# A Strassen second product whose operand sums, fifth product and first chunk are put in another order

## The chip, the cores and the metric

The kernel runs on one core of one Trainium2 chip. The metric is the time of one execution on the device in microseconds (us), as the median of several runs. Engines are named as in the profile: PE is the matrix engine (PEld its weight loads), DVE the vector engine, ACT the scalar engine, POOL the GpSimd engine, SP the sync engine, which here only starts DMAs. Each engine takes its instructions in the order in which the program gives them, and DMAs are started from the queues of SP, ACT and POOL.

## The reference

Attention over 8 batches of 8 heads, 576 positions and 64 dimensions, then a two-layer block with squared ReLU. Heads 0 to 3 see a sliding window of 32 positions, heads 4 to 7 a dilated one (every fourth position, 32 of them).

```python
scores = (1 / sqrt(64)) * q @ k.T            # per batch and head, masked
attn = exp(scores - max) / sum               # mask: sliding (h < 4) or dilated
x = (attn @ v).transpose(0, 2, 1, 3).reshape(4608, 512)
h = x @ w_in                                 # 512 -> 2048
out = (maximum(h, 0) ** 2) @ w_out           # 2048 -> 512
```

Inputs and output are float32; the kernel multiplies in float16 and sums in float32.

## The kernel before, in words

**Two streams.** For batch b the attention part writes 576 columns of `xT` (512 x 4608, float16). The two matrix products of the second part take 512 tokens at a time: nine chunks, c = 0 to 8. The program is written out by hand: a chunk's products are a Python generator, `pump(n)` takes n steps of it, and the attention of the next batch is recorded between the pumps. So while attention of batch b runs, the products of chunk b - 1 fill PE. Chunks 7 and 8 have no attention beside them.

**First product of a chunk** (`mm1_gen`). For each of 16 blocks of 128 hidden units (`ffc`), four matmuls of 512 columns write a PSUM tile `ph`; ACT applies ReLU into `rt`, and the square goes to `g`, for two blocks at once on DVE, for blocks 14 and 15 apart. One pair of blocks (`BY_ACT`, blocks 6 and 7) is squared by ACT.

**Second product** (`mm2_strassen_gen`, chunks 1 to 8). It is Strassen's scheme with seven products of half size (16 matmuls of 256 columns each) in place of eight. The left operands are blocks of `g`, or four sums of such blocks, `s1` to `s4` in the tile `sm`, made on DVE by `hidden_sums` (`s2` needs `s1`, `s4` needs `s2`). The right operands are blocks of `w_out` or four differences of them (`T`). There are four PSUM tiles: `poa`, `pod`, `pob`, `poc`. The order of the products is a (into `poa`), d (`pod`), b (`pob`), a again, b again, c (`poc`), c again. The second product of c adds to the first in the same PSUM tile, and the value after the first is needed too: DVE adds it to `u3` for the lower half of the output (line 393) before the second may start. The sums of `g` are made in three parts of the eight block pairs: pairs 0 to 3 after block 10, pairs 4 and 5 after block 13, pairs 6 and 7 after block 15 (`SUMS_AT`). Chunk 0 has no Strassen: `mm2_by_rows_gen` makes the four row blocks `po` with 64 matmuls of 512 columns; its results leave in two DMAs (`ot`, line 337), from the POOL queue.

**Attention.** For batches 0 and 1, q and k are loaded, cast to float16 and transposed on PE (`pt`, `pd`). From batch 2 on, `keep_qk` has POOL start four DMAs that write a float16 copy of q and k to DRAM (`dk`, line 184), and SP starts DMA transposes from there into `QKTx` and `QKTd` (lines 194, 196). Scores are `ps` (sliding) and `pz` (dilated); ACT takes the exponential, DVE multiplies by the mask (line 490). The product with v is `pav` or `paw`, DVE normalizes, PE transposes (`px`, `py`) and ACT copies into `xT`.

**The beginning.** PE runs matmuls on zeros (`idle`) between the pieces of attention of batch 0. Then batch 1's inputs are loaded, the first product of chunk 0 runs whole (its 512 tokens need all of batch 0), with batch 1's transposes and scores between its steps; then `mm2_by_rows_gen(0)` with batch 1's `attn_values`. After the second of its steps, DVE sets a one-word tile `hold`; POOL sets it too after that, and only then starts `keep_qk(2)`. This is how POOL's DMAs are kept back until DVE has reached a place.

Of the kernel before, what the change touches and what calls it, by code (L numbers as in the profile page):

```python
# [13 lines left out]
P = 128  # L14
# [3 lines left out]
def kernel(  # L18
# [255 lines left out]
    def hidden_sums(g, sm, i0, i1):  # L274
# [4 lines left out]
        nc.vector.tensor_add(s1, a21, a22)  # L279
        nc.vector.tensor_sub(s2, s1, a11)  # L280
        nc.vector.tensor_sub(s3, a11, a21)
        nc.vector.tensor_sub(s4, a12, s2)


    BY_ACT = (3,)
    SUMS_AT = {10: (0, 4), 13: (4, 6), 15: (6, 8)}

    def relu_squared(c, ffc, g, ph, rts):
# [5 lines left out]
        if i == NK - 1:  # L294
            nc.vector.tensor_mul(g[:, ffc, :], rt[:, o, :], rt[:, o, :])  # L295
        elif o == 1 and i in BY_ACT:
            nc.scalar.activation(g[:, ffc - 1 : ffc + 1, :], rt, ACTF.Square)
        elif o == 1:
            nc.vector.tensor_mul(g[:, ffc - 1 : ffc + 1, :], rt, rt)  # L299

    def mm1_gen(c, g, sm=None):
        xs = xT[:, :, c * TOKC : (c + 1) * TOKC]
        rts = {}
        for ffc in range(NFF):
# [12 lines left out]
            if sm is not None and ffc in SUMS_AT:  # L317
                hidden_sums(g, sm, *SUMS_AT[ffc])
# [20 lines left out]
    def mm2_strassen_gen(c, g, sm):  # L339
# [20 lines left out]
        def part(name):  # L360
            return osb.tile([P, 2, HM], FP32, name=f"{name}{c}", tag="u", bufs=3)
# [23 lines left out]
        yield  # L385
        yield from product(b_, sm[:, 2], T[:, 2], False)
# [3 lines left out]
        yield  # L390
        c_ = bank("poc")
        yield from product(c_, sm[:, 0], T[:, 0], True)
        nc.vector.tensor_add(otl[:, :, HM:DM], c_, u3)  # L393
# [232 lines left out]
    def begin(b, fill, wide=False):  # L626
        for hp in range(2):
            for i in (1, 0):
                t_sliding(b, hp, i, wide)
                fill()  # L630
        for g in range(2):
            s_sliding(b, g)
            fill()
            for i in (1, 0):
                t_dilated(b, g, i, wide, eng=nc.scalar)
                fill()
        for g in range(2):
# [24 lines left out]

    cast_sliding_qk(0, (nc.scalar, nc.scalar, nc.vector, nc.gpsimd))
# [6 lines left out]
    n_idle = [0]  # L670

    def idle():
        n_idle[0] += 1
        idle_matmuls(pj, 5, P)

    begin(0, idle)

    def idle_and_load():  # L680
        idle()
        if n_idle[0] == 15:
            nc.vector.memset(sq[:, :, :, 0:1], 0.0)
            nc.vector.memset(nd_[:, :, :, 0:1], 0.0)

    attn_values(0, idle_and_load)
# [7 lines left out]
    g0 = hidden(0)  # L694
# [90 lines left out]
```

## Time and profile before

| | |
|---|---|
| median of 13 runs | 351.83 us (349.87 to 354.18) |
| the profiled execution | 349.96 us |
| its span in the trace | 348.2 us |
| outside the span | 1.76 us |
| granted clock of PE, mean | 0.97 |
| busy: PE, DVE, ACT, POOL | 304.9, 205.5, 184.0, 48.4 us |
| moved by DMA | 47.89 MB in 82767 packets |

A row of the profile's groups gives the line, the engine and the operation, output and inputs by the program's names, the shape, how often, then the busy time and the mean of one in ns, then the idle time of the engine just before such instructions and who ended it. A row of the timeline has the start and the duration in us ahead of that. PE's busy time is counted from pipelined matmuls: one of 512 columns is shown with some 380 ns, but 64 of them in a row take 13.98 us.

### The profile page before, as it was taken

To read this page: it belongs to the slowest core of one execution; us is meant where nothing else is said; L and a number is where in the kernel's file an instruction comes from. 1 tells how busy PE (TensorE), PEld (TensorE's weight loads), DVE (VectorE), ACT (ScalarE), POOL (GpSimd) and SP (SyncE) were. 2 spreads that over 40 slices of the span, in tenths; PEclk is the share of its full clock that TensorE was granted. 3 is DMA by queue.
4 is the path that set the end of the run, shared out by engine and by line. 5 is a ranking of instruction groups with operands and counts; after the bars stand their busy time and mean duration, and the time that the engine had idled before them with its cause. 6 is when DMAs were issued, how large, how long until landed. Compare 5 with 4: busy or idle time off the path is not lost.

```text
span 348.2 us, 6958 instructions
## 1 busy us (share of the span) xinstructions
PE 304.9 (88%) x2876; PEld 199.0 (57%) x2876; DVE 205.5 (59%) x420; ACT 184.0 (53%) x311; POOL 48.4 (14%) x83
## 2 busy tenths in 40 slices
PE   6979869996989979897989798979897989899893
PEld 2865445542675459445944496448743874575482
DVE  4484565465972597359735854496538852933632
ACT  2644792378527942794279424962397227404710
POOL 4441752004004000400030002100000000000000
PEclk9869999998999999999999899998999999999999
DMA  8999999799996994599549962997110011003003
GB/s 185 206 203 242 200 181 218 180 189 200 215 187 183 206 228 51 145 199 199 102 136 198 208 102 78 222 188 158 60 63 0 2 57 65 0 2 120 2 0 121
DMA packets 82767, 47.89 MB, mean 138 GB/s; under 512 B 67760, under 2 KB 78512, under 8 KB 82352
## 3 DMA queue, kind: packets, MB, share of 16 engines
q1 hardware_dynamic: 74516, 25.99, 39.1%
q0 software_dynamic: 6848, 19.80, 26.1%
q10 hardware_dynamic: 1372, 1.67, 1.7%
q8 instruction: 22, 0.36, 0.4%
q14 instruction: 9, 0.07, 0.1%
HBM read 39.85 MB, written 16.52 MB: 162 GB/s over the span
## 4 chain that ended last, share of the span: by engine, by line
PE 42%; DVE 25%; ACT 16%; DMA 8%; issue 6%; SPq 1%; POOL 0%; ACTq 0%; DVEq 0%
PE ph L307 11%; PE poa L349 7%; PE pob L349 7%; ACT rt L293 6%; PE pod L349 5%; DVE g L299 5%; ACT AT L489 4%; PE poc L349 4%; DMA QKTx<-dk 3%; DVE x_d L551 3%; DVE AT L490 3%; DMA dk<-in_k_dram 3%; DVE sm L280 2%; ACT vd L145 2%; DMA sq<-in_k_dram 2%
## 5 line engine op out<-in xcount | busy, mean ns | idle before, releaser
L307 PE MATMUL ph<-xT,wi 128*128 128x512 f16 x576 | 133.0, 382 | 2.9 <-ACT rt L293 1.2
L293 ACT ACTIVATE rt<-ph 128x512 f16<-128x512 f32 x144 | 82.3, 609 | 22.8 <-PE ph L307 22.4
L307 PEld LDWEIGHTS <-wi 128*128 128x128 f16 x576 | 54.5, 98 | 66.2 <-issue 6.6
L299 DVE TENSOR_TENSOR g<-rt 128x1024 f16<-128x1024 f16 x54 | 38.7, 720 | 54.7 <-ACT rt L293 54.5
L349 PEld LDWEIGHTS <-sm 128*128 128x128 f16 x512 | 47.2, 98 | 14.6 <-issue 9.8
L349 PEld LDWEIGHTS <-g 128*128 128x128 f16 x384 | 37.1, 101 | 24.8 <-DVE g L295 12.5
L349 PE MATMUL poa<-wo,g 128*128 128x256 f16 x256 | 35.6, 278 | 14.5 <-DVE g L295 10.8
L349 PE MATMUL pob<-T,sm 128*128 128x256 f16 x256 | 32.5, 272 | 0.0
L621 ACT COPY xT<-py 128x576 f16<-128x576 f16 x16 | 10.2, 638 | 40.3 <-PE py L615 40.3
L603 ACT COPY xT<-px 128x576 f16<-128x576 f16 x16 | 10.2, 640 | 39.0 <-PE px L597 39.0
L490 DVE TENSOR_TENSOR AT<-AT,maskp 128x576 f16<-128x576 f16 x32 | 18.6, 585 | 19.5 <-ACT AT L489 18.3
L365 POOL DMA_DIRECT2D out_dram<-otl x6 | 4.5, 756 | 169.8 <-DVE otl L393 152.1
L489 ACT ACTIVATE AT<-pz 128x576 f16<-128x576 f32 x32 | 19.5, 695 | 15.7 <-PE pz L536 15.7
L349 PE MATMUL poc<-wo,sm 128*128 128x256 f16 x128 | 16.3, 272 | 8.8 <-DVE otl L393 8.8
L551 DVE TENSOR_TENSOR x_d<-paw,rcp_d 72x512 f16<-72x512 f32 x32 | 22.0, 687 | 1.1
L489 ACT ACTIVATE AT<-ps 128x576 f16<-128x576 f32 x32 | 19.2, 662 | 0.0
L435 PE MATMUL pj<-zz 128*128 128x128 f16 (+1 forms) x124 | 18.1, 295 | 1.2 <-DVE zz L208 1.2
L349 PE MATMUL pod<-T,g 128*128 128x256 f16 x128 | 18.4, 297 | 0.0
L551 DVE TENSOR_TENSOR x_p<-pav,rcp_p 96x512 f16<-96x512 f32 x24 | 16.5, 687 | 0.8
L349 PE MATMUL poc<-T,sm 128*128 128x256 f16 x128 | 16.2, 272 | 0.0
L322 PE MATMUL po<-wo,g 128*128 128x512 f16 x64 | 15.8, 379 | 0.0
L550 DVE RECIPROCAL rcp_d<-paw 72x8 f32<-72x8 f32 x32 | 6.4, 199 | 15.5 <-PE paw L582 15.5
(89 smaller groups left out, 341.5 us busy)
## 6 DMA issues: line engine op xcount, KB each, us to landing
sv<-in_v_dram SPq DMA_DIRECT2D x40, 128.0 KB, 10.3
sd<-in_v_dram SPq DMA_DIRECT2D x7, 512.0 KB, 8.5
dk<-in_k_dram POOLq DMA_DIRECT2D x12, 288.0 KB, 8.0
dk<-in_q_dram POOLq DMA_DIRECT2D x12, 288.0 KB, 9.1
out_dram<-otl POOLq DMA_DIRECT2D x6, 512.0 KB, 3.3
out_dram<-otu POOLq DMA_DIRECT2D x6, 512.0 KB, 4.1
wi<-in_moe_w_in_dram POOLq DMA_DIRECT2D x2, 1024.0 KB, 10.9
wo<-in_moe_w_out_dram POOLq DMA_DIRECT2D x4, 512.0 KB, 9.8
```

What stands on the lines that cost most here:

```text
L145: nc.scalar.copy(o, i)
L293: nc.scalar.activation(rt[:, o, :], ph[:], ACTF.Relu)
L299: nc.vector.tensor_mul(g[:, ffc - 1 : ffc + 1, :], rt, rt)
L307: nc.tensor.matmul(ph, wi[:, dmk, ffc * P : ffc * P + P], xs[:, dmk, :], start=(dmk == 0), stop=(dmk == NDM - 1),)
L322: nc.tensor.matmul(po, g[:, ffc, t * P : (t + 1) * P], wo[:, ffc, :], start=(ffc == 0), stop=(ffc == NFF - 1),)
L349: nc.tensor.matmul(acc[:, t, :], lhs[:, k, t * P : (t + 1) * P], rhs[:, k, :], start=(first and t == 0 and k == 0), stop=(k == NK - 1), sk ...
L435: nc.tensor.matmul(pj[:, 0:cols], zz[:, 0:P], zz[:, 0:cols], start=True, stop=True)
L489: nc.scalar.activation(AT[:, u, 0:UW], ps[:, :, 0 : UW // 2], ACTF.Exp, scale=scale)
L490: nc.vector.tensor_mul(AT[:, u, 0:UW], AT[:, u, 0:UW], mask)
L551: nc.vector.tensor_tensor(out=x[0:w], in0=pv[:, :, :, 0:D], in1=rcp[0:w].unsqueeze(3).to_broadcast([w, 2, HH, D]), op=ALU.mult,)
L603: nc.scalar.copy(xT[:, 0:2, t0 : t0 + 288], px[:, 0:UW].rearrange("x (c t) -> x c t", c=2),)
L621: nc.scalar.copy(xT[:, 2:4, t0 : t0 + 288].rearrange("x c (i r) -> x c i r", r=DIL), py[:, 0:UW].rearrange("x (c r i) -> x c i r", c=2, r= ...
```

## The change

Two things are changed in the products, and the beginning is written anew.

- The four sums of pairs 0 to 3 are recorded one at a time, after blocks 8, 9, 10 and 11. Those of pairs 4 to 7 come all four after block 15. The pair that ACT squared is squared by DVE.
- In the second product, the first product of c comes before the second of b; ACT copies its result to SBUF (`v5`), and the output's lower half is made from `v5`. The pool that holds `s1`, `u2`, `u3` has four buffers, for `v5`.
- Chunk 0's first product is made in two parts, tokens 0 to 287 and 288 to 511 (`mm1_part_gen`). The first part starts when the attention values of the first 288 positions of batch 0 are there; the rest of that batch's attention is recorded between its steps. The casts of batch 0's v on POOL change places (dilated first, then the loads of `w_in`, then sliding); batch 1's casts go from POOL to ACT and DVE; `w_out` is loaded after a `hold`; the dilated scores of batch 1 move into `mm2_by_rows_gen(0)`, with larger pumps; the loads of v for batch 2 wait for a memset on DVE; in batch 2 four steps more of chunk 1 are pumped ahead of the scores.

```diff
@@ hidden_sums, relu_squared
-        nc.vector.tensor_add(s1, a21, a22)
-        nc.vector.tensor_sub(s2, s1, a11)
-        nc.vector.tensor_sub(s3, a11, a21)
-        nc.vector.tensor_sub(s4, a12, s2)
-    BY_ACT = (3,)
-    SUMS_AT = {10: (0, 4), 13: (4, 6), 15: (6, 8)}
+        yield nc.vector.tensor_add(s1, a21, a22)
+        yield nc.vector.tensor_sub(s2, s1, a11)
+        yield nc.vector.tensor_sub(s3, a11, a21)
+        yield nc.vector.tensor_sub(s4, a12, s2)
...
-        elif o == 1 and i in BY_ACT:
-            nc.scalar.activation(g[:, ffc - 1 : ffc + 1, :], rt, ACTF.Square)
         elif o == 1:
             nc.vector.tensor_mul(g[:, ffc - 1 : ffc + 1, :], rt, rt)
+    def mm1_part_gen(c, g, t0, t1):
+        xs = xT[:, :, c * TOKC + t0 : c * TOKC + t1]
...
@@ mm1_gen
-            if sm is not None and ffc in SUMS_AT:
-                hidden_sums(g, sm, *SUMS_AT[ffc])
+            if sm is not None and ffc >= NFF // 2:
+                if ffc == NFF // 2:
+                    sums = hidden_sums(g, sm, 0, NK // 2)
+                if ffc == NFF - 1:
+                    sums = hidden_sums(g, sm, NK // 2, NK)
+                for _ in sums:
+                    if ffc < NFF - 1:
+                        break
@@ mm2_strassen_gen
+        c_ = bank("poc")
+        yield from product(c_, sm[:, 0], T[:, 0], True)
+        v5 = part("v5")
+        nc.scalar.copy(v5, c_)
+        yield
         yield from product(b_, sm[:, 2], T[:, 2], False)
         u3 = part("u3")
         nc.vector.tensor_add(u3, b_, s1)
         nc.vector.tensor_add(otl[:, :, 0:HM], d_, u3)
-        yield
-        c_ = bank("poc")
-        yield from product(c_, sm[:, 0], T[:, 0], True)
-        nc.vector.tensor_add(otl[:, :, HM:DM], c_, u3)
+        nc.vector.tensor_add(otl[:, :, HM:DM], v5, u3)
         put(1, otl, out_eng)
@@ the beginning
-    cast_sliding_v(nc.gpsimd, 2, 0, 2)
+    cast_dilated_v(nc.gpsimd, 2)
     load_w_in()
-    cast_sliding_v(nc.gpsimd, 2, 2, NB)
-    cast_dilated_v(nc.gpsimd, 2)
+    cast_sliding_v(nc.gpsimd, 2)
...
     load_sliding_qk(1)
     load_v(1)
     load_dilated_qk(1)
-    cast_sliding_qk(1, (nc.gpsimd,) * 4)
-    load_w_out()
-    cast_sliding_v(nc.gpsimd, 2)
-    cast_dilated_v(nc.gpsimd, 2)
     g0 = hidden(0)
-    pending.append(mm1_gen(0, g0))
-    pump(22)
-    begin(1, lambda: pump(1))
+    pending.append(mm1_part_gen(0, g0, 0, 288))
...
+    pump(1000)
+    pending.append(mm1_part_gen(0, g0, 288, TOKC))
+    pump(2)
+    nc.vector.memset(hold, 0.0)
+    nc.gpsimd.memset(hold, 0.0)
+    load_w_out()
+    pump(1)
+    cast_sliding_qk(1, (nc.scalar, nc.vector, nc.scalar, nc.vector))
+    pump(2)
+    transposes_and_scores(1, lambda: pump(1))
     pump(1000)
+    cast_v(nc.scalar)
     pending.append(mm2_by_rows_gen(0, g0))
-    pump(4)
+    pump(3)
+    scores_dilated(1, lambda: pump(3))
...
         if n_val[0] == 2:
             nc.vector.memset(hold, 0.0)
+            nc.vector.memset(sv[:, :, :, 0:1], 0.0)
+            nc.vector.memset(sd[:, :, :, 0:1], 0.0)
     attn_values(1, rows_and_load, True)
     nc.gpsimd.memset(hold, 0.0)
     dk = keep_qk(2)
@@ batch 2
             load_v(b + 1)
-            pump(4)
+            pump(8)
```

The rows below are the built programs' orders, in which `x2` stands for two equal instructions in a row and the number behind a tile's name tells its buffers apart.

On DVE, the end of the first product of chunk 2 (the first chunk with full attention beside it), from the square of a pair of blocks to that of blocks 14 and 15 (line 295 before, 292 now); lines 279 to 282 are the sums `s1` to `s4`, lines 490 and 515 the masks. Before:

```order
L299 TENSOR_TENSOR g_1587<-rt_5_1705 128x1024
L490 TENSOR_TENSOR AT<-AT,maskd 128x576 x2
L299 TENSOR_TENSOR g_1587<-rt_6_1745 128x1024
L279 TENSOR_TENSOR sm_1588<-g_1587 128x512
L280 TENSOR_TENSOR sm_1588<-sm_1588,g_1587 128x512
L281 TENSOR_TENSOR sm_1588<-g_1587 128x512
L282 TENSOR_TENSOR sm_1588<-g_1587,sm_1588 128x512
L295 TENSOR_TENSOR g_1587<-rt_7_1763 128x512 x2
```

Now:

```order
L294 TENSOR_TENSOR g_1676<-rt_4_1762 128x1024
L280 TENSOR_TENSOR sm_1677<-sm_1677,g_1676 128x1024
L281 TENSOR_TENSOR sm_1677<-g_1676 128x1024
L294 TENSOR_TENSOR g_1676<-rt_5_1796 128x1024
L282 TENSOR_TENSOR sm_1677<-g_1676,sm_1677 128x1024
L515 TENSOR_TENSOR AT<-AT,maskd 128x576 x2
L294 TENSOR_TENSOR g_1676<-rt_6_1834 128x1024
L292 TENSOR_TENSOR g_1676<-rt_7_1848 128x512 x2
L279 TENSOR_TENSOR sm_1677<-g_1676 128x1024
```

The four half-length sums that stood between the square of blocks 12 and 13 and those of 14 and 15 are gone from there; the whole-length ones of the first half stand singly between earlier squares.

On DVE again, the end of the second product of chunk 2, from the normalization of the values (`x_d`) to the upper half's last sum; `otl` and `otu` are the output tiles. Before:

```order
L388 TENSOR_TENSOR u_1974<-pob_1867,s_1822 128x512
L389 TENSOR_TENSOR otl_1778<-pod_1824,u_1974 128x2x256
L550 RECIPROCAL rcp_d_0_1987<-paw_1_0_1977 72x8
L551 TENSOR_TENSOR x_d_0_1986<-paw_1_0_1977,rcp_d_0_1987 72x512
L550 RECIPROCAL rcp_d_1_2009<-paw_1_1_1999 72x8
L551 TENSOR_TENSOR x_d_1_2008<-paw_1_1_1999,rcp_d_1_2009 72x512
L393 TENSOR_TENSOR otl_1778<-poc_1990,u_1974 128x2x256
L398 TENSOR_TENSOR otu_1777<-poc_1990,u_1897 128x2x256
```

Now:

```order
L575 RECIPROCAL rcp_d_1_2093<-paw_1_1_2083 72x8
L576 TENSOR_TENSOR x_d_1_2092<-paw_1_1_2083,rcp_d_1_2093 72x512
L416 TENSOR_TENSOR u_2104<-pob_1952,s_1907 128x512
L417 TENSOR_TENSOR otl_1863<-pod_1909,u_2104 128x2x256
L418 TENSOR_TENSOR otl_1863<-v_2060,u_2104 128x2x256
L423 TENSOR_TENSOR otu_1862<-poc_2030,u_1982 128x2x256
```

The sum that read `poc` reads ACT's copy `v` now, and the three sums of the lower half stand together behind the last normalization.

On POOL, the place where batch 2's q and k are started (`dk`, line 184), with the outputs of chunk 0 (`ot`, line 337 before, 360 now) and `hold`. Before:

```order
L135 DMA wo<-in_moe_w_out_dram 128x4x512 x4
L147 CAST vp<-sv 128x8x64 x3
L147 CAST vd<-sd 128x8x64 x4
L712 MEMSET hold 128x1
L184 DMA dk_1038<-in_k_dram 16x9216
L184 DMA dk_1038<-in_q_dram 16x9216
L184 DMA dk_1038<-in_k_dram 16x9216
L184 DMA dk_1038<-in_q_dram 16x9216
L337 DMA out_dram<-ot_0_1059 128x2x512
L337 DMA out_dram<-ot_2_1071 128x2x512
```

Now:

```order
L739 MEMSET hold 128x1
L135 DMA wo<-in_moe_w_out_dram 128x4x512 x4
L360 DMA out_dram<-ot_0_1112 128x2x512
L761 MEMSET hold 128x1
L184 DMA dk_1143<-in_k_dram 16x9216
L184 DMA dk_1143<-in_q_dram 16x9216
L184 DMA dk_1143<-in_k_dram 16x9216
L184 DMA dk_1143<-in_q_dram 16x9216
L360 DMA out_dram<-ot_2_1162 128x2x512
```

The first output of chunk 0 stands ahead of `hold` and of the four copies now, where both outputs stood behind them.

More of the change, by code (lines that the diff above doesn't have):

```diff
@@ L689 @@
     load_dilated_qk(1)
[L690 to L697 removed]
+    g0 = hidden(0)
+    pending.append(mm1_part_gen(0, g0, 0, 288))
+    zs = []
+    for a in range(2):
+        pump(1)
+        zs.append(av_dilated(0, 1, a))
+    pump(1)
+    x_sliding(0, 1, xs, False)
+    pump(2)
+    x_dilated(0, 1, zs, False)
+    pump(1000)
[3 more added lines that the diff above has]
+    nc.gpsimd.memset(hold, 0.0)
+    load_w_out()
+    pump(1)
+    cast_sliding_qk(1, (nc.scalar, nc.vector, nc.scalar, nc.vector))
+    pump(2)
+    transposes_and_scores(1, lambda: pump(1))
     pump(1000)
+    cast_v(nc.scalar)
     pending.append(mm2_by_rows_gen(0, g0))
[L700 removed]
+    pump(3)
+    scores_dilated(1, lambda: pump(3))
     n_val = [0]
[L702 removed]
     def rows_and_load():
```

56 lines of the change are left out of this document (42 added, 14 removed).

## The prediction, on record before the result

> **What bounds the kernel now.** I read the engines' shares first, then PE's groups with their idle time, then the timeline where that idle time lies, the granted clock by stretches, and the chain of waits at the beginning. The engines' line of the page:
>
> ```profile
> PE 304.9 (88%) x2876; PEld 199.0 (57%) x2876; DVE 205.5 (59%) x420; ACT 184.0 (53%) x311; POOL 48.4 (14%) x83
> ```
>
> PE carries the run, and no other engine comes near. So a change pays where PE stands still. Over the whole run two groups of the second product show it:
>
> ```profile
> L349 PE MATMUL poa<-wo,g 128*128 128x256 f16 x256 | 35.6, 278 | 14.5 <-DVE g L295 10.8 <-DVE g L299 3.8
> L349 PE MATMUL poc<-wo,sm 128*128 128x256 f16 x128 | 16.3, 272 | 8.8 <-DVE otl L393 8.8
> ```
>
> 14.5 us are lost before `poa` (the first product of a waits for squares) and 8.8 us before the second product of c (it waits until DVE has read `poc`): 1.8 and 1.1 us in each of eight chunks. In the timeline, chunk 3's first wait:
>
> ```profile
> 153.58 1.00 DVE L490 TENSOR_TENSOR AT<-AT,maskp 128x576 f16<-128x576 f16 x2 [2.15 <-ACT AT L489]
> ...
> 158.25 0.82 PE L349 MATMUL poa<-wo,g 128*128 128x256 f16 x6
> ...
> 158.45 0.60 ACT L293 ACTIVATE rt<-ph 128x512 f16<-128x512 f32 x1 [0.20 <-PE ph L307]
> 159.08 0.68 DVE L299 TENSOR_TENSOR g<-rt 128x1024 f16<-128x1024 f16 x1
> 159.69 0.42 DVE L279 TENSOR_TENSOR sm<-g 128x512 f16<-128x512 f16 x1
> 159.82 0.28 PE L349 MATMUL poa<-wo,g 128*128 128x256 f16 x1 [0.76 <-DVE g L299]
> 161.15 0.75 DVE L295 TENSOR_TENSOR g<-rt 128x512 f16<-128x512 f16 x2
> 161.62 0.28 PE L349 MATMUL poa<-wo,g 128*128 128x256 f16 x1 [1.52 <-DVE g L295]
> ```
>
> PE does six of the first eight matmuls, then waits for the squares of blocks 12 and 13, and again for block 14. ACT's last ReLU ends at 159.05, so block 14's input (one ReLU earlier) was there by 158.45. DVE was late: between 159.69 and 161.15 it made sums that nobody needed yet. DVE had idled 2.15 us before 153.58.
>
> The two chunks without attention, and the end:
>
> ```profile
> 302.52 1.16 PE L349 MATMUL poa<-wo,g 128*128 128x256 f16 x9 [1.34 <-DVE g L295]
> ...
> 341.69 1.91 PE L349 MATMUL poc<-wo,sm 128*128 128x256 f16 x16 [0.78 <-DVE otl L393]
> 343.63 0.76 DVE L402 TENSOR_TENSOR otu<-poc,u 128x256 f32<-128x256 f32 x2 [2.00 <-PE poc L349]
> ```
>
> **Sums and squares, per chunk.** The durations:
>
> ```profile
> L299 DVE TENSOR_TENSOR g<-rt 128x1024 f16<-128x1024 f16 x54 | 38.7, 720 | 54.7 <-ACT rt L293 54.5
> L280 DVE TENSOR_TENSOR sm<-sm,g 128x1024 f16<-128x1024 f16 x8 | 5.5, 692 | 0.3
> L389 DVE TENSOR_TENSOR otl<-pod,u 128x512 f32<-128x512 f32 x8 | 5.5, 691 | 0.3
> L384 ACT COPY otu<-poa 128x512 f32<-128x512 f32 x8 | 4.7, 585 | 16.4 <-PE poa L349 16.4
> ```
>
> The four sums of 159.69 to 161.15 (1.46 us) leave the path. The first half's sums (4 x 0.69) move up by some two blocks, one into the idle 2.15 us; DVE gains one square there (0.72). With one sum (0.69) less in the way, and with the mask of 153.58 some 0.4 us earlier because ACT squares nothing ahead of it, DVE comes to blocks 12 and 13 at about 158.0 instead of 159.08, and without the 1.46 us it squares block 14 right behind, done at 159.1; PE wants it at about 159.0. So 0.1 to 0.4 us of the 2.28 stay; I take 0.3 per chunk: 14.5 - 8 x 0.3 = **12.1 us gained**. Nothing is gained if DVE is behind for another reason (a rival below); the most is 14.5. The second half's sums now cost 2.8 us in a row behind the last square. Their first reader is the third product, two products (32 matmuls) later; `s2` is the second of the four, 1.4 us in. Behind them on DVE wait the mask and the normalizations of the values, whose PSUM pair PE needs back: 1.1 us later against the squares, which are 2 us earlier. Bounds 0 and 0.5 us, I take 0.2 in six chunks with attention: **-1.2**.
>
> **The fifth product.** PE's wait before the second product of c goes: between the end of c's first product and its second lie 16 matmuls of b, some 1.9 us by the row of 341.69, and ACT's copy takes 0.59 like the one on line 384. **+8.8 us.** If ACT were late by more than 1 us, part came back; it waits 16.4 us for PE before the sibling copy, so it is idle there. In the last chunk the three sums of the lower half (3 x 0.69 after b) now run during c's last 1.9 us, and the last two pieces (0.76) start some 0.5 us later: **-0.5**.
>
> **The clock follows the waits.** Stretches, with PE's granted clock third from the end:
>
> ```profile
> 190.00:196.00 6.00, 4.46 (x23) 2.06 (x22) 5.93 (x13) 3.92 (x8) 0.00 (x0) 1.00 1.08 204
> 197.70:200.70 3.00, 3.00 (x16) 2.07 (x15) 1.64 (x5) 1.37 (x3) 0.00 (x0) 0.50 1.13 255
> ...
> 234.90:238.70 3.80, 3.80 (x30) 2.92 (x28) 2.10 (x6) 0.94 (x2) 0.00 (x0) 0.55 0.93 206
> ```
>
> Twice the clock falls to half right behind the two waits of a chunk (before 196, PE was busy 4.46 of 6 us). That costs 3.0 x 0.5 + 3.8 x 0.45 = 3.2 us, and without the waits it should not happen: **+3.2** (0 to 3.2). [...]
>
> **The beginning** is where I expect a loss. The chain that brings batch 2's keys and queries:
>
> ```profile
> 57.02 1.03 POOL dk L184 x2
> 58.05 8.96 DMA dk<-in_k_dram
> 67.03 2.13 SPq L194
> 69.26 12.13 DMA QKTx<-dk
> 81.53 0.67 PE ps L517 x12
> ```
>
> and the timeline beside it:
>
> ```profile
> 56.78 0.10 POOL L712 MEMSET hold<- 128x1 f32 x1 [8.23 <-DVE hold L708]
> ...
> 68.46 0.77 POOL L337 DMA_DIRECT2D out_dram<-ot  x1 [9.31 <-ACT ot L334]
> 69.11 9.23 PE L307 MATMUL ph<-xT,wi 128*128 128x512 f16 x42
> ...
> 85.02 0.53 POOL L184 DMA_DIRECT2D dk<-in_k_dram  x1
> 95.00 5.72 SPq L194 DMA_TRANSPOSE QKTx<-dk  x2
> ```
>
> Copies start at 57.02, transposes at 67.03, and PE, which begins chunk 1 at 69.11 and runs out at 78.3, waits until 81.53. In the new order of POOL's queue the first output of chunk 0 (`ot_0`) stands ahead of `hold` and the copies. It is complete only 0.65 us before chunk 0 ends (68.46 against 69.11), and POOL waits for it in order: here it already did, 9.31 us. So the copies cannot start before about the end of chunk 0 plus 0.1 us, some 11.5 us later than now.
>
> Does chunk 0 end earlier? At the beginning:
>
> ```profile
> 15.15 1.52 POOL L128 DMA_DIRECT2D wi<-in_moe_w_in_dram  x2
> ...
> 18.06 2.28 POOL L147 CAST vd<-sd 128x512 f16<-128x512 f32 x4
> ...
> 31.02 9.23 PE L307 MATMUL ph<-xT,wi 128*128 128x512 f16 x42 [0.29 <-ACT xT L621]
> 36.76 3.53 POOL L147 CAST early<-sq 96x768 f16<-96x768 f32 x4 [9.25 <-DMA sq<-in_k_dram]
> ...
> 40.09 0.42 PE L460 MATMUL pt<-ident,early 96*128 96x96 f16 x6
> ...
> 51.68 0.31 PE L536 MATMUL pz<-QKTd 64*128 64x72 f16 x8 [2.43 <-ACT AT L489]
> ```
>
> The first part of the product can start before 31.02, since of the ten value steps of batch 0 four now come behind its start; I estimate 4 us. But batch 1's transposes need its q and k, which landed at 36.76, and the loads of `w_in` ahead of them now stand behind four casts (2.28 us). The casts, halved between ACT and DVE, take 1.8 us where POOL took 3.53. Both together leave the transposes near 40. At that place 20 matmuls of 512 columns remained, 10,240 columns; now 11 blocks of 4 x 224, 9,856. So the early start is spent waiting. Behind it ACT casts v, in three instructions, ahead of the exponentials that `pz` waits for, which makes the wait of 2.43 rather longer; row products lie around it. I take chunk 0's end at 68.5, between 66.5 and 70.5.
>
> From the copies' start to the scores it takes 24.5 us in the first case (57.02 to 81.53); in the second, 10.0 (85.02 to 95.00), then half of 5.72 and the landing:
>
> ```profile
> QKTx<-dk SPq DMA_TRANSPOSE x2, 5.7
> ```
>
> which is 18.6. The first shared the DMA engines with both outputs of chunk 0, the next one with one of them: I take 21. Scores at 68.6 + 21 = 89.6, 8.1 us later. Two blocks more are pumped ahead of them, 8 matmuls at 9.23/42 = 0.22, 1.8 us of PE time that is saved behind. **-6.3 us**, bounds -1.9 (end at 66.5, 18.6 us) and -11.8 (70.5, 24.5 us).
>
> **Sum.** 12.1 - 1.2 + 8.8 - 0.5 + 3.2 - 6.3 = 16.1 us off the profiled execution's 349.96: 333.9. That execution is the second shortest of the 13; most of their scatter I put down to dips of the clock, of which fewer remain, so I add nothing: **334 us**. Its own bounds: gains between 16 and 25, loss between 2 and 12, so 327 to 346 at the extremes.
>
> **Rivals.**
> (A) The beginning costs nothing: q and k of batch 1 come early enough that chunk 0 ends by 63, and the scores come at 82 to 84. For it speaks the start 4 us earlier, against it that the loads decide and `w_in` is later. It gives 334 - 6 = 328.
> (B) DVE takes half back. In the stretch before 196 it is busy 5.93 of 6 us, the chunk shrinks by 3 us, and the longer block of sums, the masks and the normalizations stand in one queue. If the values' PSUM tiles come back late in each chunk, half of the 22.4 us of steady gain goes: 334 + 11 = 345. Against it speaks that DVE's share over all is 59%.
> (C) Slower: keys and queries become late in every chunk, since POOL starts the copies for the next batch only behind the last output of the chunk before.
>
> ```profile
> 127.17 0.98 PE poa L349 x8
> ...
> 162.27 0.98 PE poa L349 x8
> ```
>
> A chunk takes 35.1 us by these rows of the chain, shortened some 32, and from the copies' start to the scores that use them lies at least one chunk. Copy and transposes take 18.6 to 24.5 us, so a reserve of 7 us stays. It decides from 32 us on; at 39 five chunks would lose 7 each, 334 + 35 = 369, and it is slower than before from 36 on.
> (D) The product's order changes nothing because the waits only change their name (block 14 then waits for ACT): only the fifth product's 8.8 less the loss of 6.3, some 347. ACT loses a square per chunk and its ReLU for block 14 was in time, so this too is unlikely.
>
> **How the numbers follow.** The forecast 0.62, A 0.13, B 0.15, C 0.04, D 0.06. The likeliest case alone is 329 to 340. The range reaches to A below and into B above: 327 to 343. About 0.5% (1.8 us) is what a measurement of this kernel can tell from no change; below 350.1 lie all but C and a small part of D: faster 0.94, same 0.02, slower 0.04.
>
> **What would show it.** The idle time before `poa` should fall from 14.5 to under 4 us, the one before the second product of c to under 1; no half clock near the middle of the run. POOL's row for `ot_0` should show a long wait, the first copy for batch 2 should start at 66 to 71, and PE should wait 8 to 14 us before the first `ps` on `QKTx`. It is wrong if the copies start near 57, if chunk 0 ends before 64, if a chunk with attention still takes over 34 us, or if PE waits for `QKTx` again in later chunks.

## The result and the profile after

| | before | after |
|---|---|---|
| median | 351.17 us of 48 runs (347.33 to 355.24) | 330.97 us of 11 runs (330.01 to 333.45) |
| ratio | | 0.945, 95% interval 0.943 to 0.948 |
| profiled execution, its span | 349.96, 348.2 us | 330.57, 328.8 us |
| a chunk with attention beside it | 35.1 us | 31.85 us |

The ratio compares the means without the few slower executions of the kernel before, so it is not the quotient of the two medians. The changed kernel is 5.5% faster, 3.0 us below the forecast of 334 and inside its range. PE's groups of the second product and of the two places that wait for attention, in the changed kernel (line 372 is 349 of before, 542 is 517, 640 is 615; the columns are busy time and mean ns, then idle time and what ended it):

```profile
L372 PE MATMUL poa<-wo,g 128*128 128x256 f16 x256 | 32.6, 273 | 0.0
L372 PE MATMUL poc<-wo,sm 128*128 128x256 f16 x128 | 16.3, 273 | 0.0
L372 PE MATMUL poc<-T,sm 128*128 128x256 f16 x128 | 16.2, 272 | 2.1 <-ACT otu L407 2.1
L607 PE MATMUL paw<-vd,AT 128*128 128x65 f16 x256 | 13.4, 194 | 1.2 <-DVE x_d L576 0.7 <-DVE x_p L576 0.6
L640 PE MATMUL py<-ident,x_d 72*128 72x72 f16 x128 | 7.2, 197 | 1.3 <-DVE x_d L576 1.1
L542 PE MATMUL ps<-QKTx 64*128 64x96 f16 x144 | 5.7, 216 | 4.9 <-DMA QKTx<-dk 4.9
```

Both waits of before, 14.5 and 8.8 us, are gone. In their place stand a wait of 2.1 us before the first product of c, some 1.9 us more before `paw` and `py` (0.4 and 0.2 before the change), and a longer wait for batch 2's transposed keys (4.9 us for 3.2). The chain of waits shows the chunk's period, from the second eight matmuls of `poa` in one chunk to those of the next two:

```profile
128.33 0.98 PE poa L372 x8
...
160.17 0.98 PE poa L372 x8
...
192.03 0.98 PE poa L372 x8
```

In the middle the granted clock (third column from the end) no longer falls; the stretches that held the two dips of before read 0.72 there and now:

```profile
196.00:202.00 6.00, 5.55 (x75) 4.89 (x74) 3.44 (x10) 1.76 (x3) 0.00 (x0) 1.00 0.93 186
234.00:240.00 6.00, 6.00 (x74) 4.96 (x73) 4.90 (x9) 3.12 (x4) 0.77 (x1) 1.00 0.02 3
```

The timeline of the changed kernel where batch 2's keys and queries are brought:

```profile
57.48 4.70 SPq L106 DMA_DIRECT2D sv<-in_v_dram  x6
...
66.80 0.72 POOL L360 DMA_DIRECT2D out_dram<-ot  x1 [25.67 <-ACT ot L357]
...
67.55 0.53 POOL L184 DMA_DIRECT2D dk<-in_k_dram  x1
...
76.07 5.80 SPq L194 DMA_TRANSPOSE QKTx<-dk  x2
...
84.58 0.67 PE L542 MATMUL ps<-QKTx 64*128 64x96 f16 x12 [4.88 <-DMA QKTx<-dk]
```

Chunk 0 ends at 67.61, the copies start at 67.55, and the first scores of chunk 1 come at 84.58, where they came at 81.53. Behind that wait the clock is at half, by the view of stretches:

```profile
80.00:82.00 2.00, 0.00 (x0) 0.00 (x0) 2.00 (x5) 0.52 (x2) 0.00 (x0) 1.00 1.09 240
82.00:84.00 2.00, 0.00 (x0) 0.00 (x0) 0.68 (x2) 0.00 (x0) 0.00 (x0) 0.86 1.19 237
84.00:86.00 2.00, 1.42 (x14) 0.76 (x15) 0.28 (x1) 0.96 (x2) 0.18 (x1) 0.50 1.06 204
...
90.00:92.00 2.00, 2.00 (x19) 1.27 (x15) 1.44 (x4) 1.87 (x4) 1.85 (x4) 0.93 0.90 204
```

Worked out from the mean of a stretch, the clock is at half from 83.4 to 90.3, and once more from 110.8 to 114.2. The kernel before had one such stretch there, from 81.3 to 84.7.

**Where the time came from.** Up to chunk 1's first scores the changed kernel is 3.05 us later (84.58 against 81.53), up to chunk 2's 3.8 (117.83 against 114.05). From there to the end it takes 210.97 us instead of 234.15, 23.2 less. Together that is the 19.4 us between the spans.

### The profile page after: what moved, and what is told of

Its sections match the earlier page's. It is cut to its first block, busy times and chain, and to the rows that moved or that the text cites. A ratio compares the mean times of both kernels' runs of the same rounds, so it can differ in the third digit from the quotient of the medians.

```text
span 328.8 us, 7031 instructions
## 1 busy us (share of the span) xinstructions
PE 300.6 (91%) x2920; PEld 200.6 (61%) x2920; DVE 207.0 (63%) x409; ACT 188.3 (57%) x331; POOL 38.9 (12%) x73
## 4 chain that ended last, share of the span: by engine, by line
PE 71%; DMA 11%; ACT 10%; DVE 2%; issue 2%; SPq 1%; POOL 1%; ACTq 0%; DVEq 0%
PE ph L324 28%; PE poa L372 9%; PE pob L372 9%; PE poc L372 7%; DMA wi<-in_moe_w_in_dram 4%; PE pod L372 4%; PE po L345 3%; ACT vd L145 3%; DMA sq<-in_k_dram 2%; ACT vp L145 2%; DMA dk<-in_k_dram 2%; PE ph L302 2%; PE paw L607 2%; PE pav L593 2%; PE ps L542 2%
## 5 line engine op out<-in xcount | busy, mean ns | idle before, releaser
L324 PE MATMUL ph<-xT,wi 128*128 128x512 f16 x512 | 119.6, 388 | 1.9 <-ACT rt L290 1.6
L290 ACT ACTIVATE rt<-ph 128x512 f16<-128x512 f32 x128 | 73.8, 602 | 23.5 <-PE ph L324 19.3
L324 PEld LDWEIGHTS <-wi 128*128 128x128 f16 x512 | 49.5, 100 | 61.7 <-issue 8.1
L372 PEld LDWEIGHTS <-g 128*128 128x128 f16 x384 | 35.9, 98 | 5.9
L372 PE MATMUL poa<-wo,g 128*128 128x256 f16 x256 | 32.6, 273 | 0.0
L628 ACT COPY xT<-px 128x576 f16<-128x576 f16 x16 | 10.2, 640 | 30.7 <-PE px L622 30.7
L515 DVE TENSOR_TENSOR AT<-AT,maskp 128x576 f16<-128x576 f16 x32 | 15.4, 482 | 11.9 <-ACT AT L514 10.5
L646 ACT COPY xT<-py 128x576 f16<-128x576 f16 x16 | 10.2, 638 | 18.6 <-PE py L640 18.5
L302 PE MATMUL ph<-xT,wi 128*128 128x288 f16 (+1 forms) x128 | 16.9, 272 | 2.6 <-DMA wi<-in_moe_w_in_dram 1.0
L575 DVE RECIPROCAL rcp_d<-paw 72x8 f32<-72x8 f32 x32 | 6.5, 203 | 19.5 <-PE paw L607 19.4
L515 DVE TENSOR_TENSOR AT<-AT,maskd 128x576 f16<-128x576 f16 x32 | 13.8, 465 | 5.2 <-ACT AT L514 4.8
L576 DVE TENSOR_TENSOR x_p<-pav,rcp_p 96x512 f16<-96x512 f32 x24 | 16.5, 687 | 0.8
```

Source lines behind the costliest of these rows:

```text
L290: nc.scalar.activation(rt[:, o, :], ph[:], ACTF.Relu)
L302: nc.tensor.matmul(ph[:, 0 : t1 - t0], wi[:, dmk, ffc * P : ffc * P + P], xs[:, dmk, :], start=(dmk == 0), stop=(dmk == NDM - 1),)
L324: nc.tensor.matmul(ph, wi[:, dmk, ffc * P : ffc * P + P], xs[:, dmk, :], start=(dmk == 0), stop=(dmk == NDM - 1),)
L372: nc.tensor.matmul(acc[:, t, :], lhs[:, k, t * P : (t + 1) * P], rhs[:, k, :], start=(first and t == 0 and k == 0), stop=(k == NK - 1), sk ...
L515: nc.vector.tensor_mul(AT[:, u, 0:UW], AT[:, u, 0:UW], mask)
L576: nc.vector.tensor_tensor(out=x[0:w], in0=pv[:, :, :, 0:D], in1=rcp[0:w].unsqueeze(3).to_broadcast([w, 2, HH, D]), op=ALU.mult,)
```

## The experiments

Theory at the start: the two edits of the products bring what the prediction says and lose nothing to each other, and the new beginning costs about 6 us because the copies of batch 2's q and k stand behind an output in POOL's queue. Each edit was first made alone on the kernel before. Where the beginning's loss was larger than the theory allowed, it was taken apart.

### The sums and squares alone

The kernel before with the new `hidden_sums`, its new places, and DVE's square for blocks 6 and 7:

```
-    BY_ACT = (3,)
-    SUMS_AT = {10: (0, 4), 13: (4, 6), 15: (6, 8)}
...
+            if sm is not None and ffc >= NFF // 2:
+                if ffc == NFF // 2:
+                    sums = hidden_sums(g, sm, 0, NK // 2)
+                if ffc == NFF - 1:
+                    sums = hidden_sums(g, sm, NK // 2, NK)
```

> The kernel before with the sums and squares of the change alone (first half of the sums one by one after blocks 8 to 11, second half after block 15, all squares on DVE). My account: the idle time before poa goes from 14.5 us to under 1, the 8.8 us before the second product of c stay, and the two half-clock stretches near 197 and 235 us go because the waits ahead of them go: 14.5 + 0 to 3.2 us less, so 333.5 to 337. Rival, the waits only change their name (blocks 14 and 15 wait for ACT, or DVE is late for another reason): 343 or more. Rival on the clock, the dips do not hang on these waits: the idle time falls by 14 us but two half-clock stretches stay in the middle, 336 to 338.

Measured: 326.88 us, ratio 0.928 (0.924 to 0.933), 24.7 us less than before in the same job and 6.6 below the expected range. This edit alone beats the whole change. The groups of this kernel:

```profile
L350 PE MATMUL poa<-wo,g 128*128 128x256 f16 x256 | 32.4, 273 | 0.0
L350 PE MATMUL poc<-wo,sm 128*128 128x256 f16 x128 | 16.3, 272 | 8.8 <-DVE otl L394 8.8
```

The wait before `poa` is gone entirely, and the group's busy time fell too, from 35.6 to 32.4. Idle and busy together are 17.7 us less, where the prediction had 12.1. The chunk's period is 32.7 (120.55 to 153.25), and the clock stays whole from 56 us to PE's last matmul. Between the two spans lie 22.4 us: what the 17.7 leave is mostly the clock, whose three stretches at half behind 80 us are gone, and chunk 1's first scores, at 79.7 for 81.53. The waits before `paw` and `py` are 0.4 and 0.2, as before.

### The fifth product alone

```
+        c_ = bank("poc")
+        yield from product(c_, sm[:, 0], T[:, 0], True)
+        v5 = part("v5")
+        nc.scalar.copy(v5, c_)
...
-        nc.vector.tensor_add(otl[:, :, HM:DM], c_, u3)
+        nc.vector.tensor_add(otl[:, :, HM:DM], v5, u3)
```

> The kernel before with the fifth product early and copied by ACT, alone. My account: the 8.8 us before the second product of c go, about 2.1 us come back as a new wait of c's first product for ACT's copy of poa (as in the changed kernel), the 14.5 us before poa stay: 343.5 to 346. The half-clock stretches behind the poa waits should stay, one to three of them. Rival, c's first product finds its PSUM tile free here and nothing comes back: 341 to 343.

Measured: 343.34 us, ratio 0.975 (0.971 to 0.980), 8.2 us less than before in the same job and 0.2 below the expected range. Its groups:

```profile
L349 PE MATMUL poa<-wo,g 128*128 128x256 f16 x256 | 34.9, 274 | 16.4 <-DVE g L295 11.8 <-DVE g L299 4.6
L349 PE MATMUL poc<-wo,sm 128*128 128x256 f16 x128 | 16.3, 272 | 0.0
L349 PE MATMUL poc<-T,sm 128*128 128x256 f16 x128 | 16.2, 272 | 2.1 <-ACT otu L384 2.1
```

The 8.8 us go. The wait for `otu`, which is ACT's copy of `poa` out of PSUM, comes with this edit and not with the sums: c's first product now stands one product earlier and takes the slot that this copy frees, 0.42 us in each of five chunks. The wait before `poa` is 1.9 us longer than in the kernel before.

### Both, with the old beginning

> The kernel before with sums, squares and the fifth product, and the old beginning. My account, in which the new beginning loses 3 to 4 us by the place of the second chunk's scores: faster than the changed kernel, 326 to 329. Rival, the new beginning is worth its place (the early start of chunk 0's product pays): 331 or more.

The edit is the two above together. Measured: **321.23 us**, ratio 0.913 (0.907 to 0.918), 4.8 below the expected range. This is 9.7 us below the changed kernel, which differs from it only in the beginning. The two agree from chunk 2 on: the period is 31.86 us here (118.89 to 150.75) and 31.85 there. In the one, chunk 2's second eight matmuls of `poa` run at 118.89, in the other at 128.33; 9.4 of the 9.8 us between the spans are there. The timeline of this kernel, to be read against the one of the changed kernel above:

```profile
55.94 0.54 POOL L184 DMA_DIRECT2D dk<-in_k_dram  x1
...
65.06 7.20 SPq L194 DMA_TRANSPOSE QKTx<-dk  x2
...
77.19 0.43 PE L520 MATMUL ps<-QKTx 64*128 64x96 f16 x12
```

No wait for keys stands before these scores, and the clock is whole from 16 us to PE's last matmul. Chunk 0 ends at 68.03: the new beginning, which starts the first product 2.6 us earlier (25.52 against 28.09 here), ends chunk 0 only 0.4 us earlier.

### The new beginning alone

The kernel before with `mm1_part_gen`, the new beginning and `pump(8)`.

> The kernel before with the new beginning alone. My account: the copies of batch 2's q and k start near 67.5 us in place of 57, PE waits some 5 us for QKTx, chunk 1 runs behind by 3 to 4 us from there to the end: 353 to 356. Rival, the new beginning gains: below 349.

Measured: 354.03 us, ratio 1.009 (1.005 to 1.013): slower by 0.9%, as expected. The first scores of chunk 1 come at 87.2 against 81.53. So the beginning costs some 3 us beside the old products and 9.7 beside the new ones. In the profiled executions the old beginning itself is not the same, though the programs differ there only by a square and a few sums of chunk 1 on DVE: the transposes of `QKTx` took 14.5 us (before), 13.2 (sums alone), 11.8 (fifth product alone) and 10.7 (both), and the first scores came at 81.53, 79.7, 77.9 and 77.19. These 4.3 us (81.53 to 77.19), read from one execution each, are most of the difference between the two prices. Why the transposes vary stays open.

### The copies ahead of the first output

The changed kernel with `hold` and the copies recorded at the second value step:

```
             nc.vector.memset(sd[:, :, :, 0:1], 0.0)
+            nc.gpsimd.memset(hold, 0.0)
+            dks.append(keep_qk(2))
...
-    nc.gpsimd.memset(hold, 0.0)
-    dk = keep_qk(2)
```

> The changed kernel with POOL's hold and the four copies of batch 2's q and k recorded at the second step of batch 1's values, so ahead of the first output of chunk 0 in POOL's queue. My account, the output in front of the copies is what the beginning costs: copies at about 57.5 us, QKTx there at 77 to 81, PE waits under 2.5 us before the first scores in place of 4.9, the long half-clock stretch behind that wait shrinks or goes, 321 to 324. Rival, the loads of v for batch 2, which now run at the same time as the copies, hold the transposes back: 328 or more.

Measured: 329.31 us, ratio 0.939 (0.934 to 0.945). The theory falls, in this form; the rival, loads that hold the transposes back, fits. The timeline of this kernel:

```profile
58.65 6.91 SPq L106 DMA_DIRECT2D sv<-in_v_dram  x6
58.85 0.54 POOL L184 DMA_DIRECT2D dk<-in_k_dram  x1
...
68.35 0.37 SPq L114 DMA_DIRECT2D sd<-in_v_dram  x1
...
68.82 14.59 SPq L194 DMA_TRANSPOSE QKTx<-dk  x2
...
86.11 0.67 PE L542 MATMUL ps<-QKTx 64*128 64x96 f16 x12 [5.23 <-DMA QKTx<-dk]
```

The copies start 8.7 us earlier than in the changed kernel, but the scores come 1.5 us later. The transposes started 7.3 us earlier and needed 17.3 us in place of 8.5. Ahead of them in SP's queue, and beside the copies, are the loads of batch 2's values. The new beginning lets them start only at 58 us, behind DVE's two `memset`s of `sv` and `sd`; in the old one they were started from 44.62.

### The order of the casts and the loads of `w_in`

The changed kernel with the casts of batch 0's v in the old order, so that the loads of `w_in` are started earlier:

```
-    cast_dilated_v(nc.gpsimd, 2)
+    cast_sliding_v(nc.gpsimd, 2, 0, 2)
     load_w_in()
-    cast_sliding_v(nc.gpsimd, 2)
+    cast_sliding_v(nc.gpsimd, 2, 2, NB)
+    cast_dilated_v(nc.gpsimd, 2)
```

> The changed kernel with the old order of batch 0's casts on POOL, so that w_in is loaded some 1.7 us earlier. My account: PE's wait of 1.0 us for w_in goes, but batch 1's q and k and the copies behind the output decide, so 329.5 to 331. Rival, the loads of w_in set the beginning: 328 or less.

Measured: 329.44 us, ratio 0.942 (0.935 to 0.948), which overlaps the changed kernel's. The first scores are at 84.33 against 84.58. PE's wait of 1.0 us for `w_in` is gone, as expected, and the time is at the lower edge of the expected range. This order is not where the beginning's loss lies.

### Uneven steps between the value pieces, with the copies ahead

The copies ahead, as above, and the steps between the value pieces of later batches dealt unevenly:

```
-        attn_values(b, lambda: pump(2))
+        steps = iter((2, 2, 2, 2, 2, 0, 4, 2, 2, 2))
+        attn_values(b, lambda: pump(next(steps)))
```

> As e5_early, and in the chunks with attention the first product of c is pumped one piece of attention later and whole, so that a transpose and one product of values stand between poa's last matmul and it. My account, c waits for the PSUM tile that ACT's copy of poa sets free (0.42 us in each of five chunks): 2.1 us shrink to under 1, so 1 to 1.5 us under e5_early. Rival, the wait moves on to the products of values (their PSUM pair): no difference within 0.7 us, or slower.

Measured: 329.12 us, 0.938 (0.934 to 0.942). The wait before c's first product fell from 2.1 to 0.8 us over the run; against the run with the copies ahead (329.31) the total did not move by what can be told.

### The square given back to ACT

The changed kernel with blocks 6 and 7 squared by ACT again.

> The changed kernel with the square of blocks 6 and 7 given back to ACT. My account, the places of the sums are what gained and the square fell into idle time of DVE: 330 to 332, as the changed kernel, idle time before poa still under 1.5 us. Rival, the square's move carries a part of it, since ACT then lags behind PE: 333 or more.

Measured: 333.04 us, 0.949 (0.943 to 0.955), at the edge of the rival's range and not in that of the account; the interval overlaps the changed kernel's. Its group of `poa`:

```profile
L374 PE MATMUL poa<-wo,g 128*128 128x256 f16 x256 | 34.3, 273 | 0.4
```

0.4 us of idle and 1.7 of busy time come back, 2.1 together, and the period is 32.09 us (132.21 to 164.30 in the chain), 0.24 longer. The median is 2.1 higher too, but in the profiled execution 3.3 us lie in the first scores already (87.85), so the time alone proves nothing. By the rows, the order of the sums carries the gain and the square moved to DVE adds some 2 us.

### The loads of batch 2's values released, with the copies ahead

The kernel with the copies ahead, less the two `memset`s that hold the loads:

```
-            nc.vector.memset(sv[:, :, :, 0:1], 0.0)
-            nc.vector.memset(sd[:, :, :, 0:1], 0.0)
```

> The changed kernel with the copies at the second value step (as in the run that moved them) and without the two memsets of sv and sd at that step, which hold the loads of batch 2's values until 57 to 58 us. What the memsets write is written again by the loads, so the work is whole. Theory, loads held: the loads then start behind ACT's casts of the values of batch 1, at 48 to 52 us, in the stretch 52 to 58 us where the transfers stand idle; the transposes no longer queue behind them (in the run with early copies the loads' issue lasted from 58.65 to 68.72, and the transposes took 17 us); they start at 66 to 69 and take 8 to 11 us, the first scores of chunk 1 at 76 to 80 against 86.1, no half clock there, and the median is 319 to 324. Rival, transposes slow whenever they come beside the outputs of chunk 0 and the copies: first scores at 84 or later and 327 to 331.

Measured: 324.76 us, ratio 0.926 (0.922 to 0.931); the median is 0.8 above the expected range, and 4.6 us below the run with the copies ahead, whose interval it does not touch. The timeline:

```profile
50.78 6.15 SPq L106 DMA_DIRECT2D sv<-in_v_dram  x6
...
59.56 0.54 POOL L184 DMA_DIRECT2D dk<-in_k_dram  x1
...
67.97 8.21 SPq L194 DMA_TRANSPOSE QKTx<-dk  x2
...
78.83 0.30 POOL L776 CAST hold<-QKTx 128x1 f32<-128x1 f16 x1 [7.33 <-DMA QKTx<-dk]
...
81.72 0.43 PE L542 MATMUL ps<-QKTx 64*128 64x96 f16 x12
```

The transposes start where they did in the run with the copies ahead (67.97 against 68.82) and need 10.9 us instead of 17.3 (16.6 in the run with the uneven steps, which has the copies ahead as well). So the loads did not only hold up the start of the transposes, they were still being moved beside them: with the copies ahead, SP started the 512 KB load of `sd` at 65.67, and loads of this kind took 6.4 us to land there (median of two): by that it was moved until some 72.1, and the transposes had started at 68.82. The keys are there at 78.83, before PE asks for them; PE's wait is gone, and so is the half clock behind it. The scores still come 1.7 us behind the expected 76 to 80, since chunk 0 ends only at 69.69 in this execution.

### The loads released, the copies left behind the output

The changed kernel less the same two lines.

> The changed kernel without the two memsets of sv and sd alone; the copies stay behind the first output of chunk 0, at 67 to 69 us. Theory, both orders hold the beginning: the loads move into the idle stretch before 58 us, but the transposes still wait for the copies' last byte (76 us in the changed kernel), so the first scores stay at 82 to 85 and the median at 328 to 331.5. Rival, the loads alone cost what the beginning lost: first scores at 80 or earlier and 322 to 326.

Measured: 332.43 us, 0.949 (0.943 to 0.954), no faster than the changed kernel, as the theory said; but the median is 0.9 above its range and the first scores, at 88.12, come 3 us behind it. The transposes then wait for the copies, as in the changed kernel, where SP stands 12.9 us for `dk`:

```profile
69.39 0.53 POOL L184 DMA_DIRECT2D dk<-in_k_dram  x1
...
79.54 5.84 SPq L194 DMA_TRANSPOSE QKTx<-dk  x2
...
88.12 0.67 PE L542 MATMUL ps<-QKTx 64*128 64x96 f16 x12 [6.57 <-DMA QKTx<-dk]
```

Of the 3.5 us by which these scores come later than in the changed kernel, 1.8 stand at chunk 0's end already (69.45 for 67.61). So each of the two edits alone brings little or nothing (1.7 us less and 1.5 more than the changed kernel's median, with intervals that overlap its own), and both together 6.2 us. Two holds stand one behind the other: the copies behind chunk 0's first output, and the loads of the values behind two `memset`s.

### Both edits of the products, old beginning, uneven steps

> The new sums and squares and the early fifth product with the beginning of the kernel before (321.2 us when it ran), and with the blocks of the product between the value steps of the later chunks dealt 2,2,2,2,2,0,4,2,2,2 instead of 2 each. In the run where this table stood beside early copies it took the wait before the third product from 2.1 to 0.8 us in a chunk and the whole run stayed the same, within 1.3 us. Theory, the wait only moves: 320 to 322.5, same as without the table. Rival, what was gained there was lost by chance in the beginning: 318 to 320.

The edit is the one with the uneven steps, on the kernel with both edits and the old beginning. Measured: 320.66 us, ratio 0.916 (0.909 to 0.923). The group shows that less of the wait is left:

```profile
L350 PE MATMUL poc<-T,sm 128*128 128x256 f16 x128 | 15.4, 272 | 0.8 <-ACT otu L385 0.8
```

The two kernels with the old beginning can't be told apart by time; either beats the kernel before by some 30 us and the changed one by some 10.

### Two blocks fewer ahead of the scores

The changed kernel with `pump(4)` in place of `pump(8)` in batch 2.

> The changed kernel with pump(4) in place of pump(8) ahead of chunk 1's scores of batch 2, as in the kernel before: two blocks fewer of chunk 1's first product run before the scores. The prediction put 1.8 us on these two blocks. Theory, they fill a wait that stands anyway: TensorE's wait for the transposed keys grows from 4.9 by 1.7 or more, the first scores of chunk 1 stay at 84 to 88, and the two blocks are done behind them, so the median goes up from 331.0 by 1.5 to 4 (half clock behind the longer wait), to 332.5 to 335. Rival, the blocks cost nothing where they are put, because ScalarE's casts of the values hold them (TensorE stood behind the casts until 79.7 in the changed kernel): the wait grows, the rest follows with a shorter stretch at half clock, and the median is 330 to 332.

Measured: 330.46 us in six runs, ratio 0.943 (0.939 to 0.947): the rival. PE runs out earlier and waits longer:

```profile
71.79 5.99 PE L324 MATMUL ph<-xT,wi 128*128 128x512 f16 x27
85.39 0.67 PE L542 MATMUL ps<-QKTx 64*128 64x96 f16 x12 [7.61 <-DMA QKTx<-dk]
```

Chunk 2's first scores are at 117.55, against 117.83 with the two blocks ahead. The groups show where the two blocks lose again what they fill: without them `paw` and `py` wait 0.0 and 0.6 us, with them 1.2 and 1.3, and the half clock from 110.8 to 114.2 is not there without them. In the eight kernels with these two blocks ahead `paw` and `py` wait 2.1 to 3.5 us together, in the six without 0.6 to 1.1.

## Why the prediction was right, and where not

By its own steps:

**The sums and squares, 12.1 us.** The mechanism was right, the size too small by 4.4 us. The step that failed is the term itself: it counted the 14.5 us of idle time and left 2.4 of it standing. Nothing stayed, and 3.0 us of busy time went as well (35.6 to 32.6; 3.2 with the sums alone, while the fifth product alone, which keeps the waits, keeps 34.9). In the prediction's timeline two matmuls of a chunk stood alone with 0.28 us each, where sixteen in a train take 1.91, 0.12 each. Two of them in eight chunks are 16 x 0.16 = 2.6 us that the group's busy time hides. That this is the cause is worked out, not tested by itself. Another part is the clock: before, 2.1 us of `poa` (1.80 and 0.29) stand in the two half-clock stretches in the middle, and the 1.0 us lost there are also in the 3.2 below. Without them the term is 14.5 + 3.0 - 1.0 = 16.5.

**The values' PSUM pair, -1.2 us.** This came to nothing: with the sums alone `paw` and `py` wait as before. The 1.9 us more of the changed kernel stand almost whole in chunk 1, 1.8 of them at 106 to 109.5, and come from elsewhere: some 0.5 with the fifth product (0.3 and 0.8 in the run with it alone), the rest with the two blocks ahead of the scores, as the run without them shows. The new wait that does return in five chunks, 2.1 us before the first product of c, was not foreseen. The prediction asked whether ACT's copy of `poc` would be in time, and not what c's product, moved ahead of b, would find in PSUM.

**The fifth product, +8.8 and -0.5.** The 8.8 came as predicted, shown by the run with this edit alone. The end cost 1.3: from PE's last matmul to the end of the span it was 4.60 us before and is 5.92 now; 5.57 and 5.54 in the two other kernels with the early fifth product, 4.59 with the sums alone.

**The clock, +3.2.** In the profiled executions no dip is left in the middle, in this kernel or in the others that have lost the wait before `poa`; those that keep it still have one or two. The prediction's lower bound of 0, dips that stay without the waits, came in no run. What stood ahead of the dips can be read from the fourteen traces together. In the kernel before, from 26.71 us on, the stretches between two changes of the clock last 54.61, 3.41, 112.64, 3.41, 34.13 and 3.41 us, which is 16, 1, 33, 1, 10 and 1 times 3.413. In the changed kernel, from 15.19 on, they last 68.27, 6.83, 20.48, 3.41 and 211.63 us, 20, 2, 6, 1 and 62 times as much. In the other traces too the changes lie on such a grid, and ahead of PE's last matmul every stretch at half lasts 3.4, 6.8 or 10.2 us. Cut into such steps, each trace from one of its own changes, from 40 us to the last products, they give for the steps at whole clock (PE's busy time as the profile counts it):

| PE busy, share of the step | steps | at half in the next step |
|---|---|---|
| under 0.50 | 27 | 27 |
| 0.50 to 0.545 | 6 | 4 |
| above | 1061 | 0 |

Back to whole it went behind all 31 half-clock steps in which PE was busy over 0.84, and behind none of the 9 with under 0.80. So in these traces the dips do come behind the waits, but only where a step holds enough of them. Before, the step from 193.97 to 197.38 has PE busy 1.14 us (0.33) and the one from 231.52 to 234.93 1.71 us (0.499), and the clock falls at the end of both; the one from 159.83 to 163.24, with the like waits of chunk 3, has 1.89 us (0.554) and it does not. The single waits are the same in all three chunks, 0.76 and 1.52 us, and PE is busy beside them: none of these steps is idle. The dip at 110.8 in the changed kernel comes in the same way: behind waits of 0.69, 1.13 and 0.29 us, none longer, PE is busy 1.85 us (0.54) in the step from 107.35; two steps of other traces with a little less, 0.521 and 0.536, brought none. The grid lies differently in each execution: in the run with the copies ahead the clock falls at 53.3 us, in the one that has the uneven steps as well at 55.5, 0.6 of a step later. That this is why one profile has a dip where its like has none is an estimate, not tested.

**The beginning, -6.3.** As a sum it was about right: the terms as they came (16.5 - 2.1 - 0.5 + 8.8 - 1.3 + 3.2 = 24.6) leave 5.2 us for it out of 19.4, between its bounds of 1.9 and 11.8. Of its steps, chunk 0's end (67.61 for 68.5), the place of the copies behind the output (67.55 for 68.6, POOL waiting 25.67 us) and the early start spent waiting came as written. Two steps failed. From the copies to the scores it took 17.0 us, below the lower bound of 18.6, so PE waited 4.9 us and not 8 to 14. And the two blocks pumped ahead were to save 1.8 us; the run without them shows nothing saved. What was missing is the clock: at half over 6.9 and 3.4 us, of which PE worked 5.7 and 3.4, it took 4.6 us out of chunks 1 and 2 (in these two stretches a matmul of 512 columns starts every 427 ns in a row, at whole clock every 216), against 1.6 by the stretch that before had at 81.3 (3.2 us of work); the prediction had dips go and none come.

Against the same products with the old beginning the price is higher than the prediction's, 9.7 us. The products in turn gained some 30 us in that run where the sum had 22.4. That the time still came within 3.0 us of the forecast is in part luck: a gain and a loss that were both put too small. The cause that the prediction named for the loss, copies behind the output, is only one of two. The runs with the copies ahead (329.3), the loads released (332.4) and both (324.8) show that the late loads of the values are the other, and that either alone holds the beginning. The prediction read POOL's queue and not SP's: the diff shows the two `memset`s, and what they hold is the next load in SP's queue, which waits 18.3 us for DVE's `sd` in the changed kernel. The transposes and the loads share SP's queue: behind loads that were started until 68.7 the transposes needed 17.3 us, behind loads started by 58 they needed 10.9. No run parts the order in the queue from the mere sharing of the DMA engines. Of the 9.7 us, 6.2 go with both holds; 3.5 remain between 324.76 and 321.23. The traces put 3.1 of these before chunk 2's second product (121.97 against 118.89). Of the 3.1, 1.7 stand at chunk 0's end (69.69 against 68.03): the clock is at half from 55.1 to 58.5 there and not in the run with the old beginning, which is 1.7 us of work. Another 1.3 are the waits for the values in chunk 1 (0.69 and 1.13 us, against one of 0.55). This is read from one execution each, not tested.

**The rivals.** B (DVE takes half back) and C (keys late in each chunk) did not come: the period is 31.85 us, and no later chunk waits for `QKTx`. D fell with the first run. A, a beginning that costs nothing, would have been 328; the runs with the old beginning show that even this was too high by 7, since the gain of the products was larger.

## What to carry to other kernels

Idle time before an instruction group is not the whole price of a wait that comes in the middle of it: look at the group's busy time too (3.0 us here, beside 14.5 of idle), and at what the clock does behind; but count what the slow clock adds to the busy time (1.0 us here) only once. When a start is rewritten to begin earlier, follow every queue that feeds the next stage, of loads as of outputs, and count what each now stands behind: here, with two holds in a row, removing one brought 1.7 us less or 1.5 more, removing both 6.2 less. Measure the parts of a change alone: here two of three made the kernel 30 us faster, and the third gave 10 back.

## What the runs showed that was not expected

- The same two DMA transposes (`QKTx` of batch 2) took 8.3 to 8.8 us in the six kernels that start them latest, at 76 to 80; 10.1 to 14.5 in the five with the old beginning, at 65 to 67; 10.9 with early copies and early loads; and 16.6 and 17.3 right behind loads of the same queue.
- PE's long waits went on costing. In the nine executions that waited 3 us or more for batch 2's keys, the clock stayed at half for 2.9 to 6.1 us after work had started again; 5.7 us (84.58 to 90.3) behind the wait of 4.9 in the changed kernel, some 2.9 us of work.
- In these traces the clock did not go by the length of single waits: it fell behind all 27 steps of 3.41 us in which PE was busy under 0.50, and behind none of the 1061 over 0.545, in 1094 steps of fourteen traces.
